# Sketched attention feeding a ReGLU layer on one core: key products of batch 0 on GpSimd alone, z sums that start with the rest, and loads that count as work in the plan

## The chip, the cores and the metric

One core of one Trainium2 chip. The metric is the device time of one execution in us; lower is better. Executions are marked fast or slow: slow is one that is over 1.5% above the fastest of the same kernel. The profile of a kernel is one execution; its span (first to last instruction) is 1.6 to 3.3 us below the execution's time in these runs.

## The reference, cut to what matters

```python
# q, k, v: (4 batches, 4 heads, 1088, 32); S1, S2: (8, 32); x: 4352 tokens of 128; d_ff 1536
def phi(x):                               # 64 features per token and head
    a = np.einsum('rd,bhsd->bhsr', S1, x)
    b = np.einsum('rd,bhsd->bhsr', S2, x)
    return np.einsum('bhsi,bhsj->bhsij', a, b).reshape(*x.shape[:-1], r * r)
q_p, k_p = phi(q), phi(k)
kv = np.einsum('bhsf,bhsd->bhfd', k_p, v)
z = np.sum(k_p, axis=2)
x = einsum('bhsf,bhfd->bhsd', q_p, kv) / (einsum('bhsf,bhf->bhs', q_p, z)[..., None] + 1e-06)
out = (np.maximum(x @ w_gate, 0.0) * (x @ w_val)) @ w_out      # x with its heads side by side
```

## The kernel before

The core works on 102 feed-forward units. Each unit is a gate and a val matmul, a ReLU on ScalarE, a product on VectorE (`ht`) and four out matmuls. They need x, which the attention makes group by group: group 0 (half of the first half of batch 0, units 0 to 5), group 1 (units 6 to 11), group 2 (units 12 to 23), then two groups for each later batch, and one for the last 64 tokens of every batch. All attention work of batch 0 up to the first x is start-up; that of the other batches is woven between the units.

The order of instructions is fixed when the kernel is built: a list scheduler (`plan`) gives each operation a duration, dependences, a level (its priority) and a gate (the unit at which it may be placed at the earliest), and emits the operations in the order of its own clock. On the chip an engine runs its operations in that order, and semaphores make it wait.

```python
def outer(eng, dst, ab, a0, b0, n, a=None):     # line 202 is in here: both inputs lie in SBUF
    eng.tensor_tensor(out=..., in0=a_src[..., None].to_broadcast(...),
                      in1=ab[:, :, None, b0:b0 + R].to_broadcast(...), op=ALU.mult)
# ... in add_k: key products, four of 128x512 per batch; VectorE shares them for batch 0
for c in range(0, GC, 2):
    for hf in range(2):
        dve = first and hf == 0
        phis.append(op("DVE" if dve else "POOL", 640 if dve else 1080, kb.phi, hf, ...))
# ... z: four sums over the chunks, then the rest (the last 64 tokens), then a mask, w, and its fill
for c in range(GC):
    zs.append(op("PE", 330, kb.z, c, ...))
zs.append(op("PE", 500, kb.z_rest, x, deps=(zs[-1], rest_t2), level=lv, **kw))
zd = op("DVE", 200, kb.zdiag, deps=(zs[-1],), level=lv, **kw)
# ... in plan: while TensorE would idle, matmuls of zeros (line 155, "fillers") keep it busy
gap = t - clock["PE"] if o.eng == "PE" else 0
if gap > WGAP and clock["PE"] < WARM_UNTIL:
    warm(int((gap - 100) / (57 if t > 7000 else 110)))
# ... leads in units: keys and queries of a batch are spread over units s-KA..s-KB and s-QA..s-QB
K0, KA, KB, QA, QB = 2, 35, 25, 20, 8
# ... loads: placed by gates and fixed times, no duration in the plan
op("ACT", 200, load_k, b, at=13500.0, gate=[0, -1, 4, 20][b])
op("ACT", 200, load_rest_q, b, gate=[0, 0, 10, 24][b])
```

The query side (`add_q`) is, per group: transpose of q, matmul with the sketches, transpose to `abq`, `bw` (a product of two parts of `abq`), `den`, `an`, the query product `qp` (line 202 again), transposes on TensorE, `num`, and x on ScalarE. Group 0 has `bw`, `an` and `qp` on VectorE; groups 1 and 2 have `bw` and `an` on VectorE and `qp` on GpSimd; the later groups have all three on GpSimd.

## Time and profile before

| | before |
|---|---|
| time, median of 3 (range) | 125.57 us (124.8 to 126.27) |
| span of the profiled execution (a fast one of 126.52 us, not among the three), mean granted clock | 123.9 us, 0.962 |
| mask of the z sums starts (VectorE, line 318) | 13.01 us |
| query product of group 0 starts (VectorE) | 17.38 us |
| first gate matmul (line 454) | 22.11 us |
| span minus first gate, called **middle** below | 101.8 us |

The mask, the query product and the first gate say how long the start-up takes; the middle says how well the rest runs, whatever the start did.

### The profile page before, as it was taken

To read this page: it belongs to the slowest core of one execution; us is meant where nothing else is said; L and a number is where in the kernel's file an instruction comes from. 1 tells how busy PE (TensorE), PEld (TensorE's weight loads), DVE (VectorE), ACT (ScalarE), POOL (GpSimd) and SP (SyncE) were. 2 spreads that over 40 slices of the span, in tenths; PEclk is the share of its full clock that TensorE was granted. 3 is DMA by queue.
4 is the path that set the end of the run, shared out by engine and by line. 5 is a ranking of instruction groups with operands and counts; after the bars stand their busy time and mean duration, and the time that the engine had idled before them with its cause. 6 is when DMAs were issued, how large, how long until landed. Compare 5 with 4: busy or idle time off the path is not lost.

```text
span 123.9 us, 2888 instructions
## 1 busy us (share of the span) xinstructions
PE 114.9 (93%) x1117; PEld 80.6 (65%) x1117; DVE 97.3 (78%) x198; ACT 81.3 (66%) x165; POOL 46.8 (38%) x62
## 2 busy tenths in 40 slices
PE   6994899889999999999999999999999999999940
PEld 6864748767877669765665568755655766667920
DVE  3589376587889889397999796788979998979940
ACT  4100004795865649698996578659979988989930
POOL 6959102600593179941510199117005404000000
PEclk9999559999999999999999999999999999999995
DMA  2999990554053507562002100120020011011022
GB/s 49 300 141 192 181 224 6 176 107 158 9 188 55 105 0 177 77 156 100 14 0 41 49 3 0 11 79 0 3 52 33 8 28 57 5 19 65 0 44 83
DMA packets 9521, 9.28 MB, mean 75 GB/s; under 512 B 3364, under 2 KB 7844, under 8 KB 9508
## 3 DMA queue, kind: packets, MB, share of 16 engines
q1 hardware_dynamic: 5228, 6.82, 18.7%
q0 software_dynamic: 4096, 2.25, 14.2%
q8 instruction: 8, 0.13, 0.4%
q10 hardware_dynamic: 184, 0.04, 0.1%
q14 instruction: 5, 0.04, 0.1%
HBM read 9.12 MB, written 2.23 MB: 92 GB/s over the span
## 4 chain that ended last, share of the span: by engine, by line
PE 74%; DVE 11%; DMA 5%; ACT 4%; issue 2%; SPq 1%; ACTq 0%
PE bank L454 16%; PE bank L481 16%; PE bank L466 15%; PE bank L372 8%; DVE ht L471 8%; PE bank L254 5%; DMA q_sb<-in_q_dram 5%; PE bank L409 3%; ACT g_sb L460 2%; PE bank L427 2%; PE bank L302 2%; PE bank L280 2%; PE bank L334 2%; PE bank L155 2%; PE bank L312 1%
## 5 line engine op out<-in xcount | busy, mean ns | idle before, releaser
L471 DVE TENSOR_TENSOR ht<-g_sb,bank 128x512 f16<-128x512 f16 x102 | 65.7, 676 | 11.3 <-ACT g_sb L460 5.3
L460 ACT ACTIVATE g_sb<-bank 128x512 f16<-128x512 f32 x102 | 60.0, 602 | 15.7 <-PE bank L454 13.7
L481 PEld LDWEIGHTS <-ht 128*128 128x128 f16 x408 | 30.3, 98 | 18.4 <-issue 2.0
L481 PE MATMUL bank<-wo,ht 128*128 128x128 f16 x408 | 39.3, 219 | 0.6 <-DVE ht L471 0.6
L454 PE MATMUL bank<-xT,wg 128*128 128x512 f16 (+1 forms) x120 | 38.7, 347 | 0.6 <-ACT xT L433 0.5
L466 PE MATMUL bank<-xT,wv 128*128 128x512 f16 (+1 forms) x120 | 38.3, 347 | 0.4 <-DVE ht L471 0.4
L202 POOL TENSOR_TENSOR qp<-an,abq 128x1024 f16<-128x1024 f32 (+1 forms) x9 | 15.8, 1757 | 8.7 <-DVE an L397 8.1
L202 POOL TENSOR_TENSOR kp<-abk 128x512 f16<-128x512 f32 x14 | 14.5, 1064 | 8.5 <-DVE abk L265 8.5
L384 POOL TENSOR_TENSOR bw<-abq 128x128 f32<-128x128 f32 (+1 forms) x7 | 3.1, 436 | 31.7 <-DVE abq L380 31.7
L466 PEld LDWEIGHTS <-wv 128*128 128x128 f16 x120 | 11.7, 99 | 3.3 <-issue 1.6
L454 PEld LDWEIGHTS <-wg 128*128 128x128 f16 x120 | 11.5, 100 | 3.3 <-issue 2.0
L372 PE MATMUL bank<-qt,wst 128*128 128x512 f32 (+2 forms) x26 | 11.4, 553 | 0.0
L416 ACT COPY pt<-bank 128x512 f16<-128x512 f16 x17 | 10.0, 596 | 1.4 <-PE bank L409 1.4
L254 PE MATMUL bank<-kt,sk 128*128 128x256 f32 x32 | 9.6, 396 | 0.0
L380 DVE STREAM_TRANSPOSE abq<-bank 128x512 f32<-128x512 f32 (+1 forms) x10 | 6.3, 633 | 2.9 <-PE bank L372 2.9
L155 PE MATMUL bank<-zero 128*128 128x128 f16 x88 | 7.5, 256 | 1.1 <-DVE maskw L142 1.1
L155 PEld LDWEIGHTS <-zero 128*128 128x128 f16 x88 | 6.7, 117 | 1.4 <-DVE maskw L142 1.1
L246 DVE STREAM_TRANSPOSE kt<-k_sb 128x512 f32<-128x512 f32 x8 | 5.5, 698 | 1.9 <-DMA k_sb<-in_k_dram 1.9
L324 ACT ACTIVATE kv<-bank 64x64 f16<-64x64 f32 x16 | 3.5, 218 | 5.2 <-PE bank L292 5.0
L433 ACT CAST xT<-bank 128x512 f16<-128x512 f32 (+1 forms) x10 | 5.3, 529 | 2.3 <-PE bank L427 2.2
L280 PEld LDWEIGHTS <-kp 128*128 128x128 f16 x64 | 4.2, 112 | 3.5 <-DVE kp L202 1.9
L280 PE MATMUL bank<-v_sb,kp 128*128 128x64 f16 x64 | 4.8, 206 | 1.8 <-DVE kp L202 1.8
(73 smaller groups left out, 98.7 us busy)
## 6 DMA issues: line engine op xcount, KB each, us to landing
q_sb<-in_q_dram SPq DMA_DIRECT2D x4, 544.0 KB, 7.5
out_dram<-o_sb SPq DMA_DIRECT2D x7, 256.0 KB
k_sb<-in_k_dram SPq DMA_DIRECT2D x3, 512.0 KB, 4.6
v_sb<-in_v_dram POOLq DMA_DIRECT2D x4, 256.0 KB, 5.9
k_sb<-in_k_dram SPq DMA_DIRECT2D x2, 256.0 KB
wg<-in_moe_w_gate_dram POOLq DMA_DIRECT2D x1, 384.0 KB, 7.3
wv<-in_moe_w_val_dram POOLq DMA_DIRECT2D x1, 384.0 KB, 8.6
wo<-in_moe_w_out_dram POOLq DMA_DIRECT2D x1, 384.0 KB, 10.2
```

Source lines behind the costliest of these rows:

```text
L155: nc.tensor.matmul(w_ps[:, 0:128], zero, zero, start=True, stop=True)
L202: eng.tensor_tensor(out=dst.rearrange("s x (i j) -> s x i j", i=R), in0=a_src[:, :, :, None].to_broadcast([dst.shape[0], n, R, R]), in1=ab ...
L254: nc.tensor.matmul(self.ps[h0][:, lo * n * 32:(lo + w) * n * 32].rearrange("p (c x) -> p c x", c=w), sk[:, hf].rearrange("p a b f -> p (a ...
L280: nc.tensor.matmul(self.m[:, p * 64:p * 64 + 64], self.kp[:, hf, c * H + 2 * p:c * H + 2 * p + 2].rearrange("s h f -> s (h f)"), v_sb[self ...
L372: nc.tensor.matmul(self.ps[:, i * w:(i + 1) * w], wst[:, b].rearrange("p h f -> p (h f)"), self.qt.rearrange("p x t -> p (x t)")[:, i * w: ...
L380: nc.vector.transpose(self.absb.rearrange("p x f -> p (x f)"), self.ps[:, 0:n * 128])
L416: nc.scalar.copy(out=self.pt[:, lo:hi], in_=self.ps[:, lo:hi])
L454: nc.tensor.matmul(g_ps[:, y * W:(y + 1) * W], wg[:, j], xT[:, self.col:self.col + W], start=True, stop=True)
L460: nc.scalar.activation(out=self.g_sb, in_=self.g_ps, func=ACTF.Relu)
L466: nc.tensor.matmul(self.v_ps[:, y * W:(y + 1) * W], wv[:, j], xT[:, self.col:self.col + W], start=True, stop=True)
L471: nc.vector.tensor_tensor(out=self.ht, in0=self.g_sb, in1=self.v_ps, op=ALU.mult)
L481: nc.tensor.matmul(o[:, s], self.ht[:, y * W + x * 128:y * W + (x + 1) * 128], wo[:, j], start=(j == 0 and s == 0), stop=(j == NJ - 1), sk ...
```

## The change

Its intent: VectorE, on the start-up's chain, loses the two key products of batch 0 to GpSimd. The rest's z sum goes ahead of the chunks, so that the mask needn't wait for it at the end. A load becomes work of a "DMA" stream in the plan, one load after the other, and what uses it depends on it. Leads and some durations are new. So are three buffers each for the results of gate and val instead of two and four, a higher level for the kv matmuls, kv's rest right after its first chunk, and two of the four kv copies of batch 0 on VectorE. Core of the diff (cut: the start and stop flags that follow from the new order, the copy's body, durations):

```diff
-    K0, KA, KB, QA, QB = 2, 35, 25, 20, 8
+    K0, KA, KB, QA, QB = 4, 37, 26, 24, 20
+    def load(ns, eng, t, fn, *args, **kw):
+        o = op(eng, t, fn, *args, **kw)
+        return op("DMA", ns, lambda: None, deps=(o,))
 # add_k
-                                  bank=(None,) if new else banks, level=lv, **kw))
+                                  bank=..., level=(3 if h0 == 0 else 2) if first else 0, **kw))
-                dve = first and hf == 0
-                phis.append(op("DVE" if dve else "POOL", 640 if dve else 1080, kb.phi, hf,
-                               nc.vector if dve else nc.gpsimd, c, 2, deps=tuple(t2s), ...))
+                phis.append(op("POOL", 1120 if first else 1080, kb.phi, hf, nc.gpsimd, c, 2,
+                               deps=tuple(t2s), level=lo_lv, **kw))
         zs = []
+        if first:
+            zs.append(op("PE", 500, kb.z_rest, x, deps=(rest_t2,), level=lv, bank=banks, **kw))
         for c in range(GC):
...
-        zs.append(op("PE", 500, kb.z_rest, x, deps=(zs[-1], rest_t2), level=lv, **kw))
+        if not first:
+            zs.append(op("PE", 500, kb.z_rest, x, deps=(zs[-1], rest_t2), ...))
...
-                cps.append(op("ACT", 210, kb.kvcopy, g, r, deps=(kvs[-1], *cps[-1:]), ...))
+                dve = first and g == 1
+                cps.append(op("DVE" if dve else "ACT", 230, kb.kvcopy, g, r, ..., deps=(kvs[-1],), ...))
 # loads of the later batches
-            lv = (op("POOL", 900, load_main, nc.gpsimd, v_sb[b], v, b, gate=[0, -1, 10, 20][b],
-                     at=13000.0), cast)
-            op("ACT", 200, load_k, b, at=13500.0, gate=[0, -1, 4, 20][b])
-            op("ACT", 200, load_rest_q, b, gate=[0, 0, 10, 24][b])
+            k_in = (load(1650, "ACT", 200, load_k, b, at=13500.0, gate=[0, -1, 4, 20][b]),)
+            q_in = (load(1800, "ACT", 200, load_rest_q, b, gate=[0, 0, 10, 24][b]),)
+            v_in = (load(1650, "POOL", 900, load_main, nc.gpsimd, v_sb[b], v, b,
+                         gate=[0, 0, 10, 20][b], at=13000.0),)
```

More of the change, by code (lines that the diff above doesn't have):

```diff
@@ L284, in kv @@
                         v_sb[self.b][:, 2 * p:2 * p + 2, cc * D:(cc + 1) * D],
-                        start=c == 0 and hf == 0 and p == 0, stop=False,
+                        start=c == 0 and hf == 0 and p == 0, stop=c == GC - 1 and hf == 1,
                         skip_group_check=True)
@@ L295, in kv_rest @@
                         vt[rows, 2 * p:2 * p + 2, e * D:(e + 1) * D],
-                        start=False, stop=e == E - 1, skip_group_check=True)
+                        start=False, stop=False, skip_group_check=True)
         def z(self, x, c):
-            if c == 0:
+            if x is not None:
                 self.zps = bank(x)[:, 0:64]
@@ L305, in z, with z_rest @@
                 ab.rearrange("s h (a f) -> s a h f", a=2)[:, :, :, R:2 * R],
-                start=c == 0, stop=False, skip_group_check=True)
-        def z_rest(self, rest):
+                start=x is not None, stop=False, skip_group_check=True)
+        def z_rest(self, x, rest):
+            if x is not None:
+                self.zps = bank(x)[:, 0:64]
             rows = slice(32 * self.b, 32 * self.b + 32)
@@ L313, in z_rest @@
                     self.zps[:, 0:32], ab.rearrange("s h f -> s (h f)"), ab[:, :, R:2 * R],
-                    start=False, stop=e == E - 1, skip_group_check=True)
+                    start=x is not None and e == 0, stop=e == E - 1, skip_group_check=True)
         def zdiag(self):
@@ L320, in zdiag, with kvcopy @@
                 in1=maskz.rearrange("p a h j -> p (a h j)"), op=ALU.mult)
-        def kvcopy(self, g, r):
-            nc.scalar.mul(
-                out=kv16[64 * r:64 * r + 64, self.b, r].rearrange("f (p g) d -> f p g d", g=2)[
-                    :, :, g],
-                in_=self.m[64 * g:64 * g + 64, 0:128].rearrange("f (p g d) -> f p g d", p=2, g=2)[
-                    :, :, g],
-                mul=KVSCALE)
+        def kvcopy(self, g, r, eng):
+            o = kv16[64 * r:64 * r + 64, self.b, r].rearrange("f (p g) d -> f p g d", g=2)[:, :, g]
+            i = self.m[64 * g:64 * g + 64, 0:128].rearrange("f (p g d) -> f p g d", p=2, g=2)[
+                :, :, g]
+            if eng is nc.scalar:
+                eng.mul(out=o, in_=i, mul=KVSCALE)
+            else:
+                eng.tensor_scalar(out=o, in0=i, scalar1=KVSCALE, scalar2=None, op0=ALU.mult)
         def w(self, x):
@@ L508, in __init__ @@
             self.holds, self.end = [], None
-    SEM = {"PE": 220.0, "ACT": 220.0, "DVE": 250.0, "POOL": 200.0}
+    SEM = {"PE": 220.0, "ACT": 220.0, "DVE": 250.0, "POOL": 200.0, "DMA": 2000.0, "SP": 2000.0}
     SLACK = (0.0, 60.0, 60.0, 0.0)
-    BUFS = {**dict.fromkeys(range(8), 1), "g": 2, "v": 4, "o": 2, "kt": 3, "qt": 3, "abk": 2, "abq": 2, "kp": 2,
+    BUFS = {**dict.fromkeys(range(8), 1), "g": 3, "v": 3, "o": 2, "kt": 3, "qt": 3, "abk": 2, "abq": 2, "kp": 2,
             "qp": 2, "ktr": 3, "pt": 2, "g_sb": 4, "ht": 8, "bw0": 1, "bw1": 1, "an": 2, "rd": 2, "zd": 2}
@@ L589, with add_rest @@
         units += [F(*grp, i) for i in range(NJ * grp[2] // 4)]
-    T0 = {"PE": 4700.0, "DVE": 2900.0, "ACT": 5300.0, "POOL": 7900.0}
+    T0 = {"SP": 4700.0, "DMA": 16500.0, "PE": 4700.0, "DVE": 2900.0, "ACT": 5300.0, "POOL": 7900.0}
     WGAP, WARM_UNTIL = 250.0, 16000.0
-    K0, KA, KB, QA, QB = 2, 35, 25, 20, 8
-    def add_rest(n, src, at, level, gate):
+    K0, KA, KB, QA, QB = 4, 37, 26, 24, 20
+    def load(ns, eng, t, fn, *args, **kw):
+        o = op(eng, t, fn, *args, **kw)
+        return op("DMA", ns, lambda: None, deps=(o,))
+    def add_rest(n, src, at, level, gate, loaded=()):
         x = Rest(n, src)
         kw = dict(level=level, gate=gate)
-        t1 = op("DVE", 360, x.t1, at=at, **kw)
+        t1 = op("DVE", 360, x.t1, at=at, deps=loaded, **kw)
         ab = op("PE", 240, x.ab, deps=(t1, sk_fill), bank=range(7), **kw)
@@ L604, in add_rest, with add_k @@
         return x, t2, phi
-    def add_k(b, rest, landed, gate, banks, loaded, behind):
+    def add_k(b, rest, landed, gate, banks, k_in, v_in, behind):
         kb = K(b)
@@ L613, in add_k @@
         for pr in range(2):
-            t1s.append(op("DVE", 620, kb.t1, pr, at=landed[pr], deps=tuple(t1s[-1:]), level=lv, **kw))
+            t1s.append(op("DVE", 620, kb.t1, pr, at=landed[pr], deps=(*t1s[-1:], *k_in), level=lv, **kw))
         n = 2 if first else 4
@@ L622, in add_k @@
                                   deps=(*t1s[h0 // 2:(h0 + n) // 2], sk_fill, *abs_[-1:], *behind),
-                                  bank=(None,) if new else banks, level=lv, **kw))
+                                  bank=(None,) if new else banks, level=(3 if h0 == 0 else 2) if first else 0, **kw))
                     abs_.append(new[-1])
@@ L630, in add_k @@
             for hf in range(2):
-                dve = first and hf == 0
-                phis.append(op("DVE" if dve else "POOL", 640 if dve else 1080, kb.phi, hf,
-                               nc.vector if dve else nc.gpsimd, c, 2, deps=tuple(t2s), level=lo_lv, **kw))
+                phis.append(op("POOL", 1120 if first else 1080, kb.phi, hf, nc.gpsimd, c, 2,
+                               deps=tuple(t2s), level=lo_lv, **kw))
         zs = []
+        if first:
+            zs.append(op("PE", 500, kb.z_rest, x, deps=(rest_t2,), level=lv, bank=banks, **kw))
         for c in range(GC):
-            zs.append(op("PE", 330, kb.z, c, deps=(*t2s, *zs[-1:]), level=lv,
+            zs.append(op("PE", 275, kb.z, c, deps=(*t2s, *zs[-1:]), level=lv,
                          bank=(None,) if zs else banks, **kw))
-        zs.append(op("PE", 500, kb.z_rest, x, deps=(zs[-1], rest_t2), level=lv, **kw))
+        if not first:
+            zs.append(op("PE", 500, kb.z_rest, x, deps=(zs[-1], rest_t2), level=lv,
+                         bank=(None,), **kw))
         zd = op("DVE", 200, kb.zdiag, deps=(zs[-1],), level=lv, **kw)
@@ L645, in add_k @@
         for c in range(GC):
-            kvs.append(op("PE", 280, kb.kv, c, bank=(None,) if kvs else banks,
-                          deps=(*phis[c // 2 * 2:c // 2 * 2 + 2], *kvs[-1:], *loaded), level=lo_lv, **kw))
-        kvs.append(op("PE", 300, kb.kv_rest, x, vt, deps=(kvs[-1], rest_phi), level=lo_lv, **kw))
-        hold("abk", t2s[0], kvs[-2])
-        hold("kp", t2s[0], kvs[-2])
+            kvs.append(op("PE", 240, kb.kv, c, bank=(None,) if kvs else banks,
+                          deps=(*phis[c // 2 * 2:c // 2 * 2 + 2], *kvs[-1:], *v_in), level=lv, **kw))
+            if c == 0:
+                kvs.append(op("PE", 300, kb.kv_rest, x, vt, deps=(kvs[-1], rest_phi), level=lo_lv, **kw))
+        hold("abk", t2s[0], kvs[-1])
+        hold("kp", t2s[0], kvs[-1])
         cps = []
@@ L653, in add_k, with add_q @@
             for r in range(2):
-                cps.append(op("ACT", 210, kb.kvcopy, g, r, deps=(kvs[-1], *cps[-1:]), level=lo_lv, **kw))
+                dve = first and g == 1
+                cps.append(op("DVE" if dve else "ACT", 230, kb.kvcopy, g, r,
+                              nc.vector if dve else nc.scalar, deps=(kvs[-1],), level=lv, **kw))
         hold("bank", kvs[0], cps[-1])
+        for c in cps[:-1]:
+            cps[-1].deps += (c,)
         return cps[-1], wf
-    def add_q(grp, n, kv, wf, landed, gate, fast, banks):
+    def add_q(grp, n, kv, wf, landed, gate, fast, banks, q_in):
         qk = Q(*grp, n)
@@ L663, in add_q @@
         rest = grp[0] == B
-        t1 = op("DVE", 560 if rest else 40 + 145 * c, qk.t1, at=landed, **kw)
-        ab = op("PE", 1000 if rest else 60 + 110 * c, qk.ab, deps=(t1, *wf), bank=banks, **kw)
+        t1 = op("DVE", 560 if rest else 40 + 145 * c, qk.t1, at=landed, deps=q_in, **kw)
+        ab = op("PE", 1000 if rest else 60 + 215 * c, qk.ab, deps=(t1, *wf), bank=banks, **kw)
         hold("qt", t1, ab)
@@ L735, in load_rest_q, with load_rest_kv @@
         load_q(nc.sync, b)
-        if b == 1:
-            load_rest(nc.sync, kr, k, range(B))
-            load_rest(nc.sync, vr32, v, range(B))
+    def load_rest_kv():
+        load_rest(nc.sync, kr, k, range(B))
+        load_rest(nc.sync, vr32, v, range(B))
     sketch = Sketch()
@@ L748 @@
     f0 = op("DVE", 420, fill_static, deps=(s_copy,), level=1)
-    rest0 = (*add_rest(32, kr0, 6000.0, 2, -1), vr0)
-    rest = (*add_rest(128, kr, 26000.0, 0, 7), vr)
-    cast = op("ACT", 400, lambda: nc.scalar.copy(out=vr, in_=vr32), gate=9, at=29000.0)
-    kvs, wfs, xs = [], [], []
+    rest0 = (*add_rest(32, kr0, 5500.0, 2, -1), vr0)
+    cast = None
+    kvs, wfs, xs, qs = [], [], [], []
     for b in range(B):
         s = start[b, 0, 2 if b == 0 else GC]
-        lv = ()
+        k_in = v_in = q_in = ()
         if b > 0:
-            lv = (op("POOL", 900, load_main, nc.gpsimd, v_sb[b], v, b, gate=[0, -1, 10, 20][b],
-                     at=13000.0), cast)
-            op("ACT", 200, load_k, b, at=13500.0, gate=[0, -1, 4, 20][b])
-            op("ACT", 200, load_rest_q, b, gate=[0, 0, 10, 24][b])
+            k_in = (load(1650, "ACT", 200, load_k, b, at=13500.0, gate=[0, -1, 4, 20][b]),)
+            q_in = (load(1800, "ACT", 200, load_rest_q, b, gate=[0, 0, 10, 24][b]),)
+            v_in = (load(1650, "POOL", 900, load_main, nc.gpsimd, v_sb[b], v, b,
+                         gate=[0, 0, 10, 20][b], at=13000.0),)
+        if b == 1:
+            kvr = load(600, "SP", 3000, load_rest_kv, gate=0)
+            rest = add_rest(128, kr, 0.0, 0, 7, (kvr,))
+            cast = op("ACT", 400, lambda: nc.scalar.copy(out=vr, in_=vr32), gate=9, deps=(kvr,))
+            rest = (*rest, vr)
+        if b > 0:
+            v_in += (cast,)
+        qs.append(q_in)
         n0 = len(ops)
-        kv, wf = add_k(b, rest if b else rest0, [(4300.0, 5300.0), (19500.0,) * 2, (0.0,) * 2, (0.0,) * 2][b],
-                       s - 40 if b > 1 else -1, range(7), lv,
+        kv, wf = add_k(b, rest if b else rest0, (4400.0, 5600.0) if b == 0 else (0.0, 0.0),
+                       s - 40 if b > 1 else -1, range(7), k_in, v_in,
                        (first_ab,) if b == 1 else ())
@@ L774 @@
                               2 if start[grp] == 0 else 1 if g0 else 0,
-                              range(7))
+                              range(7), q_in)
                 xs.append(x)
@@ L782 @@
     x, _ = add_q(groups[-1], len(xs), tuple(kvs), tuple(wfs), 0.0, start[groups[-1]] - 20, 0,
-                 range(7))
+                 range(7), sum(qs, ()))
     xs.append(x)
```

## The prediction

> **What bounds the kernel now.** I read the page's summary by slices first, then the chain of work that ended last, then the table of windows, and last the key outer products (line 202), because the chain passes through them.
>
> The slices are 3.1 us wide:
>
> ```profile
> PE   6994899889999999999999999999999999999940
> PEclk9999559999999999999999999999999999999995
> DMA  2999990554053507562002100120020011011022
> ```
>
> Counted from 0, from slice 9 (27.9 us) on TensorE is at 90% or more. The gaps are in the slices before (slice 3, 9.3 to 12.4 us, is at 4), and in slices 4 and 5 (12.4 to 18.6 us) its clock is halved. The windows say the same in us (columns: busy time and instructions of PE, PEld, DVE, ACT, POOL, then granted clock, DMA share, GB/s):
>
> ```profile
> 10.00:12.00 2.00, 0.78 (x6) 0.60 (x5) 2.00 (x1) 0.00 (x0) 2.00 (x3) 1.00 1.04 194
> 12.00:18.00 6.00, 5.12 (x26) 3.60 (x26) 3.36 (x11) 0.19 (x1) 0.71 (x1) 0.51 1.37 213
> 18.00:22.00 4.00, 3.63 (x53) 2.68 (x53) 2.56 (x11) 1.78 (x7) 1.15 (x2) 0.89 0.05 18
> 24.00:104.00 80.00, 79.53 (x766) 53.91 (x764) 68.66 (x128) 62.49 (x127) 32.95 (x36) 1.00 0.25 62
> ```
>
> Between 24 and 104 us TensorE has 0.5 us of idle time in 80; VectorE and ScalarE have 11 and 17 us. That stretch is bound by TensorE's amount of work. Between 10 and 22 us it did little, partly at half clock: the start is where time can be won. The chain there (start, us, what):
>
> ```profile
> 9.98 0.86 DVE kp L202
> 10.84 1.56 issue
> 12.40 0.68 DVE kp L202
> 13.08 0.14 DVE zd L318
> 13.23 0.04 issue
> 13.27 1.06 PE bank L334 x4
> ...
> 14.76 1.08 PE bank L372 x2
> ...
> 16.06 2.72 PE bank L372 x4
> 18.78 0.29 PE bank L292 x4
> 19.07 1.22 PE bank L155 x20
> 20.29 0.22 PE bank L409 x4
> ...
> 21.69 0.38 ACT xT L433
> 22.07 0.04 issue
> 22.11 0.38 PE bank L454 x2
> ```
>
> L454 at 22.11 is the first gate matmul of the feed-forward part; all before it is start-up. The end of that chain is the load of q for batch 0, two key products on VectorE, the masking of the z sums (L318), w (L334), the query sketches (L372, half clock), the rest matmuls of kv (L292), filler matmuls (L155), then transposes, num and x. The key products are the surprise:
>
> ```profile
> L202 POOL TENSOR_TENSOR kp<-abk x2: 1055/1057/1059, 9.8 to 10.9; 128x512 f16<-128x512 f32 x2
> L202 DVE TENSOR_TENSOR kp<-abk x2: 680/1620/2561, 9.9 to 12.4; 128x512 f16<-128x512 f32 x2
> ```
>
> The same product takes VectorE 0.68 us in one instance and 2.56 us in the other (minimum, median, maximum). The long one began at 9.92, 0.07 us after GpSimd began its own two, and ended at 12.48, one 0.68 us after GpSimd had finished them (11.93, near enough). VectorE lost 1.9 us, and the z mask, ready to run since 10.78, stood behind it in VectorE's order until 13.01.
>
> **What the Trainium skill says.** "SBUF — State Buffer", section "Who interferes with whom": a VectorE instruction with two SBUF inputs contends with a GpSimd instruction that reads SBUF, and the later one is blocked, not slowed. The trace agrees: 2.56 us beside GpSimd, 0.68 us when GpSimd was only issuing a DMA. "TensorE: Matmul & The Clock Gate", "Part 1: The HAM clock gate", puts the clock at half after a window of some 3.4 us without enough activity. The trace agrees in kind: after only fillers and small matmuls from 8.4 to 10.8 us and an idle 1.76 us, the granted clock is 0.50 from 12 to 18.6 us. "DMA: Bandwidth & Descriptors", "Issuing engines are not separate DMA queues", says DMAs of all issuers interleave on the same 16 engines. The page's DMA row is at 9 from 3 to 19 us, while k, q, v and the weights share them, which is what the change's single DMA stream models.
>
> **The change part by part.** The kernel's order of instructions comes from a list scheduler, so every edit of a duration or gate reorders. I worked the new start by hand, with the rules of the scheduler and with durations from the trace.
>
> (1) *Up to the second head pair's transpose: about 0.* The order becomes rest ahead of the second head pair on VectorE and TensorE. But the plan still places the first query transpose at 7.0 us, ahead of the rest's second transpose, and q lands at 7.94 us. VectorE will again stand there, and the second key transpose will again end near 9.07. GpSimd's first rest product stays at 8.8 to 9.9.
>
> (2) *Key products to GpSimd: removes 3.17 us from VectorE, adds two of 1.06 us to GpSimd.* GpSimd: 9.85 + 4 x 1.04 = 14.0 us, instead of 11.93 there and 13.08 on VectorE. So the keys themselves come 0.9 us later.
>
> (3) *z path, much earlier.* z_rest goes first (8.8 to 9.4), the four chunks follow and end at about 10.6. With VectorE free, the mask runs 10.6 to 10.8 (before: 13.01 to 13.22). w at full clock took 0.53 us in later batches, though up to 0.6 us of fillers may stand ahead of it: 11.6 us. The fill of wst to 11.8, first query sketch 12.4, its transpose (0.45) to 12.9. Before, that transpose ended at 16.33: 3.4 us won.
>
> (4) *A new wait.* The next operation, bw (L384), has two SBUF inputs, and GpSimd is busy with keys until 14.0. By the wait seen above it stands until about 14.0. From the start of bw to the end of the query product, before took 18.07 - 16.36 = 1.71 us: 15.7 us now, 2.35 us earlier than 18.07.
>
> (5) *The way from the query product to the first gate.* Before: 18.07 to 22.11, 4.04 us, because L372, L292 and 20 fillers stood ahead of the transposes on TensorE. From the transposes' start at 20.13 to the gate it was 1.98 us. Now kv has its keys at 14.0, so its last matmuls end near 14.8, and the four copies, two on ScalarE beside two on VectorE (0.22 each), end near 16 to 17, just beside the copy of the transposes. TensorE should be free at 15.7. Gate: 15.7 + 0.1 + 2.0 = 17.8; I add 0.2 for fillers or a copy of kv that come a little late: 18.0 us. **Gain 22.1 - 18.0 = 4.1 us.** Of it 2.35 come from the earlier query product, the rest from TensorE's queue, including its half clock (the two L372 groups took 3.8 us, against some 1.7 at full clock: 0.86 us for 512 columns later in the chain, and the two groups have 1024).
>
> (6) *Weights and loads.* wg, wv and wo land 7.3, 8.6 and 10.2 us after 5.35, 5.89 and 6.42: 12.7, 14.5 and 16.6 us, all ahead of a gate at 18.0. The v load of batch 1 moves from 11.88 to after the first gate, which can only help the weights. q of batch 1, issued after the first gate, was moved in some 3 us (issued 22.17, rates of 244 and 339 GB/s until 25); the plan now allows 4.2 us after its first gate.
>
> (7) *Steady part: the same work.* No matmul of keys, queries or feed-forward is removed, so with TensorE 99% busy the gain of the start passes through. Query work is released 24 to 20 units ahead instead of 20 to 8, so x is earlier and attention work no longer meets the last units. In 103.8 to 108.1 the chain goes over ScalarE and VectorE for 4.2 us, where some 0.5 us are lost. Against that, denser attention may cost something. Net: -0.2 us.
>
> Sum: 125.57 - 4.1 - 0.2 = 121.3 us.
>
> **The rivals.** *A: the wait moves.* GpSimd's longer run could block VectorE until well after 14.0, or TensorE's sparse work from 10 to 14 us could again halve its clock. For it: TensorE idled just 1.76 us before the fall. Against: its queue from 11.8 on holds sketches, kv and fillers. At half clock the remaining sketches, kv, transposes and first units would cost 1.5 to 2 us: 123 us. *B: hidden by later needs.* The units after the first six need x of the second group, whose query product on GpSimd now starts at about 18.7 and again waits for operations that GpSimd's reads block. I get x for unit 12 some 6.4 us after the first gate, against 7.2 before (29.29 - 22.11) and 12 units of 0.65 us: no stall. Were it wrong by 1.5 us: about 122.5. Or q of batch 1 lands after its planned transpose and holds VectorE's queue: 1 to 2 us, 122.5 to 123. *C: the start barely counts, reordering costs.* If bunched queries starve the feed-forward of banks or of VectorE, the middle loses 2 to 4 us: 124 to 126. TensorE's 0.5 us of idle in 80 shows the old order had no such trouble, and VectorE's 11 us of room speak against it.
>
> **Range and chances.** A, B and C together push upwards; downwards there is a gate near 17.3 and up to 1 us in the tail. 8 in 10: 119.6 to 123.4. The 2% line is 125.57 x 0.98 = 123.06; only A with B, or C, reach past it: faster 0.83, same 0.15, slower 0.02.
>
> **What would show it.** Right: first L454 between 17.5 and 18.6, last key product on GpSimd at about 14.0, z mask near 10.8, bw of the first group beginning to be held from about 13 and done just after 14, clock at 1.0 from 12 to 18, TensorE still about 99% busy afterwards, and the end as much earlier as the first gate. Wrong: a low clock digit in slices 4 to 6, gaps of TensorE in 18 to 30 us, or a first gate earlier by 4 us with an end that is not.

## The result, and the profile after

| | before | after |
|---|---|---|
| time, median (range), runs | 125.92 us (124.8 to 127.82), 4 | 120.5 us (120.22 to 120.68), 4 |
| span of the profiled execution, clock | 123.9 us, 0.962 | 118.5 us, 0.993 |
| z mask starts | 13.01 us | 10.15 us |
| query product of group 0 starts | 17.38 us | 14.43 us |
| first gate matmul | 22.11 us | 17.42 us |
| middle | 101.8 us | 101.1 us |

Ratio 0.9596 (95%: 0.9522 to 0.967), faster. A ratio is the mean time of one kernel's fast runs over that of the other's of the same rounds, so not quite the ratio of the medians in the table.

The slices of after (3.0 us wide), in the same rows as in the prediction:

```profile
PE   6999879999999999999999999999999999999920
PEclk9999999999999999999999999999999999999997
DMA  1999999594202740431002100020011012011021
```

Slice 3 had a 4 for TensorE before and has a 9; the clock has no low digit. The table of windows of after says the same in us:

```profile
10.00:12.00 2.00, 2.00 (x29) 1.85 (x27) 0.42 (x2) 0.00 (x0) 2.00 (x3) 1.00 1.05 184
12.00:18.00 6.00, 4.62 (x63) 3.40 (x62) 5.40 (x17) 1.73 (x7) 2.60 (x4) 1.00 1.33 189
24.00:104.00 80.00, 80.00 (x789) 53.83 (x788) 68.60 (x128) 63.42 (x130) 32.59 (x35) 1.00 0.20 53
```

From 12 to 18 us TensorE is busy for less time than before (4.62 against 5.12 us) but runs 63 matmuls instead of 26 (20 of them fillers), at a clock of 1.00 instead of 0.51. From 24 to 104 us it has no idle time left. In 10 to 12 us VectorE is busy 0.42 instead of 2.00 us: that is the held key product gone. The chain of after up to the first gate (start, us, what):

```profile
8.45 0.56 PE bank L315 x4
9.01 1.03 PE bank L303 x8
...
10.60 0.47 PE bank L338 x4
...
11.62 0.50 PE bank L376 x2
...
12.15 0.46 DVE abq L384
12.63 1.01 DVE bw L388
...
14.43 0.70 DVE qp L202
...
15.58 1.12 PE bank L155 x20
16.70 0.28 PE bank L431 x8
...
17.42 0.38 PE bank L458 x2
```

The rest's z sum (L315) and the chunks' (L303) come first, then w (L338), the sketches of group 0 (L376), and then VectorE. L458 is the first gate. One line is longer than it should be: `bw` takes 1.01 us. In VectorE's timeline (start, us, engine, line, operation) the two `bw` of the same shape in after are

```profile
12.63 1.00 DVE L388 TENSOR_TENSOR bw<-abq 128x64 f32<-128x64 f32 x1
15.66 0.21 DVE L388 TENSOR_TENSOR bw<-abq 128x64 f32<-128x64 f32 x1
```

and GpSimd's timeline has the key products of batch 0 in one piece, from 9.42 to 13.55 us, followed by a load's issue:

```profile
9.42 4.13 POOL L202 TENSOR_TENSOR kp<-abk 128x512 f16<-128x512 f32 x4
13.50 0.83 POOL L87 DMA_DIRECT2D v_sb<-in_v_dram  x1
```

The first `bw` started inside that piece and ended 0.08 us after it; the second had no GpSimd product beside it.

One part of the earlier start is not the change's. VectorE waits for the load of q before the first query transpose. The timelines of before, of after, and of after's second profile (e12 below) at that place:

```profile
7.97 0.45 DVE L362 STREAM_TRANSPOSE qt<-q_sb 128x256 f32<-128x256 f32 x1 [0.58 <-DMA q_sb<-in_q_dram]
7.54 0.45 DVE L366 STREAM_TRANSPOSE qt<-q_sb 128x256 f32<-128x256 f32 x1 [0.43 <-DMA q_sb<-in_q_dram]
8.16 0.45 DVE L366 STREAM_TRANSPOSE qt<-q_sb 128x256 f32<-128x256 f32 x1 [0.66 <-DMA q_sb<-in_q_dram]
```

The same kernel met q at 7.54 us in one execution and at 8.16 in the other, and its first gate came at 17.42 and 18.03.

### The profile page after: what moved, and what is told of

It reads as the page before. It is cut to its first block, busy times and chain, and to the rows that moved or that the text cites. A ratio compares the mean times of both kernels' runs of the same rounds, so it can differ in the third digit from the quotient of the medians.

```text
span 118.5 us, 2939 instructions
## 1 busy us (share of the span) xinstructions
PE 110.7 (93%) x1114; PEld 78.1 (66%) x1114; DVE 95.7 (81%) x198; ACT 79.8 (67%) x163; POOL 48.8 (41%) x64
## 4 chain that ended last, share of the span: by engine, by line
PE 78%; DVE 14%; issue 2%; ACT 1%; DVEq 1%
PE bank L485 15%; PE bank L458 15%; PE bank L470 15%; DVE ht L475 11%; PE bank L254 6%; PE bank L376 6%; PE bank L155 6%; PE bank L413 3%; PE bank L303 3%; PE bank L431 3%; PE bank L315 2%; PE bank L338 2%; PE bank L280 1%; DVE bw L388 1%; PE bank L224 1%
## 5 line engine op out<-in xcount | busy, mean ns | idle before, releaser
L464 ACT ACTIVATE g_sb<-bank 128x512 f16<-128x512 f32 x102 | 59.2, 607 | 13.0 <-PE bank L458 8.5
L485 PE MATMUL bank<-wo,ht 128*128 128x128 f16 x408 | 38.8, 219 | 0.4 <-DVE ht L475 0.4
L458 PE MATMUL bank<-xT,wg 128*128 128x512 f16 (+1 forms) x120 | 38.4, 347 | 0.5 <-ACT xT L437 0.5
L202 POOL TENSOR_TENSOR kp<-abk 128x512 f16<-128x512 f32 x16 | 16.5, 1061 | 6.3 <-DVE abk L265 6.3
L458 PEld LDWEIGHTS <-wg 128*128 128x128 f16 x120 | 11.9, 100 | 3.8 <-issue 2.2
L470 PEld LDWEIGHTS <-wv 128*128 128x128 f16 x120 | 11.8, 102 | 2.8 <-issue 1.4
L376 PE MATMUL bank<-qt,wst 128*128 128x512 f32 (+2 forms) x26 | 9.4, 475 | 0.0
L493 ACT ACTIVATE o_sb<-bank 128x512 f32<-128x512 f32 (+1 forms) x10 | 5.3, 532 | 3.3 <-PE bank L485 3.3
L747 ACT CAST k_sb<-wv 1x1 f32<-1x1 f16 x3 | 0.5, 179 | 9.0 <-DMA wv<-in_moe_w_val_dram 9.0
L413 PE MATMUL bank<-ident,qp 128*128 128x128 f16 x68 | 5.4, 219 | 1.1 <-DVE qp L202 0.9
## 6 DMA issues: line engine op xcount, KB each, us to landing
wo<-in_moe_w_out_dram POOLq DMA_DIRECT2D x1, 384.0 KB, 10.6
```

What stands on the lines that cost most here:

```text
L202: eng.tensor_tensor(out=dst.rearrange("s x (i j) -> s x i j", i=R), in0=a_src[:, :, :, None].to_broadcast([dst.shape[0], n, R, R]), in1=ab ...
L376: nc.tensor.matmul(self.ps[:, i * w:(i + 1) * w], wst[:, b].rearrange("p h f -> p (h f)"), self.qt.rearrange("p x t -> p (x t)")[:, i * w: ...
L413: nc.tensor.transpose(self.ps[:, k], self.qp[:, 2 * k:2 * k + 2].rearrange("s r f -> s (r f)"), ident)
L458: nc.tensor.matmul(g_ps[:, y * W:(y + 1) * W], wg[:, j], xT[:, self.col:self.col + W], start=True, stop=True)
L464: nc.scalar.activation(out=self.g_sb, in_=self.g_ps, func=ACTF.Relu)
L470: nc.tensor.matmul(self.v_ps[:, y * W:(y + 1) * W], wv[:, j], xT[:, self.col:self.col + W], start=True, stop=True)
```

## The experiments

Twelve runs in three groups, each group on one chip with its own runs of before (medians of before: 126.56, 126.37 and 125.41 us; so a run is compared by its ratio, or by spans within a group). My theory was: the gain is the start-up's, made by the key products' move, and the other parts only keep the middle from growing. The rivals: the order of the rest or the plan's DMA stream makes the gain; or the split of the keys doesn't matter, only the hole (the idle stretch) in TensorE's work and the halved clock that the plan's wrong duration led to.

### One part at a time

**e1**: before, with the key products on GpSimd alone.

```diff
-                dve = first and hf == 0
-                phis.append(op("DVE" if dve else "POOL", 640 if dve else 1080, kb.phi, hf, ...
+                phis.append(op("POOL", 1120 if first else 1080, kb.phi, hf, nc.gpsimd, c, 2, ...
```

> The kernel before with one edit: all four key products of batch 0 on GpSimd. Theory S (the start-up decides, and the keys on GpSimd are most of it): VectorE's 2.56 us product is gone, the z mask runs near 10.9 us instead of 13.0, the clock stays at 1.0 from 12 to 18 us, the first gate comes near 18.0 us (before 22.11), time 121 to 122 us. Rival M (the new leads, buffer counts and DMA stream, that is the middle, give a good part): first gate as above or later, time 123 us or more.

Measured: 122.45, 121.65, 121.61 us fast (one slow, 123.86, and that is the profiled one: first gate 19.88, middle 102.2). Ratio 0.9643 (0.9563 to 0.9723). The fast spans are 119.8 to 120.6 us, those of before on this chip 123.3 to 125.2. This one edit makes most of the gain. The start of a fast run was not profiled; with a middle of 102.2 their spans would put the first gate at 17.6 to 18.4 us (an estimate). The edit also gives the plan the true duration of these products, so it takes away the wait and the wrong number together; e9 takes them apart.

**e2**: after, with the keys split between VectorE and GpSimd again (the edit of e1 backwards).

> The kernel after with the keys of batch 0 split again between VectorE and GpSimd, all else of the change kept. Theory S: VectorE's first key product is again held behind GpSimd's (about 2.5 us instead of 0.68), the z mask comes after 12 us, first gate 19.5 to 21 us (after: 17.42), time 122.5 to 124.5 us. Rival M: the middle keeps most of the gain, time under 122 us.

Measured: 126.78 and 127.8 us fast, two slow; ratio 1.0155 (1.0043 to 1.0268): the gain is gone, and more. The key products (minimum, median, maximum in ns) are those of before:

```profile
L202 DVE TENSOR_TENSOR kp<-abk x2: 675/1565/2455, 9.7 to 12.2; 128x512 f16<-128x512 f32 x2
```

But the first gate is at 18.74 us, only 1.3 later than in after; the middle is 106.4, 5.3 longer, with a hole at 48 to 52 us (TensorE busy 1.6 of 4 us) and a clock of 0.55 to 0.59 in the 4 us behind it; as in e4 below, the keys of batch 2 run on GpSimd (from 43.18) ahead of a query product (47.28). So e2 doesn't measure the split alone: it also met a bad order later on. e6 takes that out.

**e3**: after, with the rest's z sum last again and the old levels and times for it.

```diff
-        if first:
-            zs.append(op("PE", 500, kb.z_rest, x, deps=(rest_t2,), level=lv, bank=banks, **kw))
...
-        if not first:
-            zs.append(op("PE", 500, kb.z_rest, ...
+        zs.append(op("PE", 500, kb.z_rest, ...
-    rest0 = (*add_rest(32, kr0, 5500.0, 2, -1), vr0)
+    rest0 = (*add_rest(32, kr0, 6000.0, 2, -1), vr0)
```

> The kernel after with the rest of k and the z sums of the rest in their old place (behind the second head pair, and last in the z sums). Theory S: VectorE's wait for q at about 7.5 us and GpSimd's key products until 13.55 us set the pace in both orders, so first gate 17.4 to 17.8 and time within 0.4 us of after (120.2 to 120.9). Rival O (the order of the rest is worth something by itself): first gate 18 or later, time 121.2 or more.

Measured: ratio 0.9562 (0.9472 to 0.9653), first gate 17.49, middle 101.1: no difference from after that these runs show. The order of the rest, which the change names in its title, is worth nothing here: the mask comes 0.7 us later (10.85), but GpSimd's keys begin at 9.49 (after: 9.42) and hold `bw` to their end in either order, so the delay only shortens that wait (0.38 instead of 1.00 us). The waiting for q that was expected to set the pace doesn't stand in e3's trace. Where `bw` isn't held, as in e8, the order was not tried.

**e4**: after, with the old leads.

```diff
-    K0, KA, KB, QA, QB = 4, 37, 26, 24, 20
+    K0, KA, KB, QA, QB = 2, 35, 25, 20, 8
```

> The kernel after with the five lead constants of before (2, 35, 25, 20, 8). Theory S: first gate unchanged at 17.4 us, and what the leads bring is the 0.7 us that the end gained beyond the first gate (5.4 against 4.7 us): time 120.9 to 121.4. Rival M: 122 us or more.

Measured: ratio 0.9863 (0.9793 to 0.9934). First gate 17.19, middle 105.9: the start is as good as after's, and 4.8 us are lost later. The slices (3.1 us wide) show where:

```profile
PE   6899889999999993799999999999999999999940
PEclk9999999999999998559999999999999999999995
```

TensorE is at 3 in slice 15 (46 to 49 us), and its clock halves behind it. GpSimd's timeline in e4, then in after, at that place:

```profile
41.24 4.14 POOL L202 TENSOR_TENSOR kp<-abk 128x512 f16<-128x512 f32 x4
45.34 1.95 POOL L202 TENSOR_TENSOR qp<-an,abq 128x1024 f16<-128x1024 f32 x1
```

```profile
40.33 1.96 POOL L202 TENSOR_TENSOR qp<-an,abq 128x1024 f16<-128x1024 f32 x1
42.24 4.14 POOL L202 TENSOR_TENSOR kp<-abk 128x512 f16<-128x512 f32 x4
```

In e4 the four key products of batch 2 run ahead of the query product that the next units (batch 1) need; in after it is the other way. x for those units comes at 49.80 us in e4 and 45.78 us in after. Before had the query product first too (44.53, the keys at 47.67).

### Is it that order on GpSimd?

**e5**: e4 with one dependence more: the key products of batches 2 and 3 wait in the plan for the first query product of the batch ahead.

```diff
+    ahead = {}
-    K0, KA, KB, QA, QB = 4, 37, 26, 24, 20
+    K0, KA, KB, QA, QB = 2, 35, 25, 20, 8
-                               deps=tuple(t2s), level=lo_lv, **kw))
+                               deps=(*t2s, *((ahead[b - 1],) if b > 1 else ())), ...))
+        if grp[1] == 0 and grp[0] > 0:
+            ahead[grp[0]] = phis[-1]
```

> The kernel with the old leads (the fourth run, 124.84 us) with one more dependence: the key products of batches 2 and 3 on GpSimd wait in the plan for the first query product of the batch before. Theory G (the hole of that run at 46 to 52 us is only GpSimd's order, 4.1 us of keys of batch 2 ahead of the 1.95 us query product of batch 1): the hole is gone, x of batch 1 comes some 4 us earlier (46 instead of 50 us), clock 1.0 throughout, time 120.4 to 121.4. Rival L (the old leads as such cost, by attention work spread too late): time 122 us or more.

Measured: 120.04 us in the one fast run, span 118.1 (e4: 122.2 to 123.1); three slow runs of 126.03 to 126.57. The profile is of a slow run: first gate 23.49, but middle 100.8. The hole is gone with the old leads kept. So the leads' worth is that order. One fast run is little, but the middle of the slow one says the same.

**The slow runs.** The profile of e5 let me see what slow is here. The matmuls of line 254 (ns: minimum, median, maximum), first e5, then after:

```profile
L254 PE MATMUL bank<-kt,sk x8: 633/635/796, 6.2 to 10.6; 128*128 128x256 f32 x8
```

```profile
L254 PE MATMUL bank<-kt,sk x8: 379/379/483, 5.4 to 7.8; 128*128 128x256 f32 x8
```

From the first matmuls until about 20.5 us TensorE ran at some half of its rate (ten fillers in 1.27 us at 14.5 us, against 0.72 in after), and the first gate came 6 us later; yet the record of the granted clock says 1.00 all that time (mean of the run 0.990). It doesn't go by kernel: of four executions each, three of e5 were slow, two of e2, e6, e7, e9, e10 and e11, one of e1 and e3, none of e4, e8 and the first four of after, and one of the second four. The profile fell on a slow run in e1, e5 and e10, and all three have these long matmuls, until about 20.5 us in e5 and e10 and only to 10 us in e1, whose slow run has a span 1.5 to 2.3 us longer than its fast ones; for the other slow runs no trace shows the cause. I did not find what decides it.

**e6**: after with split keys (e2) and the dependence of e5.

> The kernel with split keys (the second run, 128.38 us) with the same added dependence. Theory G: its hole in the middle goes and what is left is its later first gate (18.74 against 17.42), time 121.5 to 122.3. Rival (split keys cost beyond the first gate): 123 us or more.

Measured: 124.93 and 126.13 us fast (spans 122.6 and 123.7; two slow); ratio 1.0177 (0.9782 to 1.0572). First gate 20.43, middle 102.2. Against e2 the middle is 4.2 us shorter and the start 1.7 later (the clock dips here in slices 4 and 5, as before; in e2 it did not). Against after the span is 4.1 us longer, 3.0 of it in the start; against e12, whose q landed at nearly the same time (8.16, here 8.05), 3.5 and 2.4. That is the price of the split as the plan of before has it, with the wrong 640 ns and, in this execution, the clock's dip, but with the later hole taken out.

### Held by GpSimd, or only badly ordered?

**e9**: before, with the one wrong number put right: the plan gives the two split key products on VectorE the mean that the profile shows.

```diff
-                phis.append(op("DVE" if dve else "POOL", 640 if dve else 1080, kb.phi, hf,
+                phis.append(op("DVE" if dve else "POOL", 1620 if dve else 1080, kb.phi, hf,
```

> The kernel before with one number changed: the plan counts VectorE's key products of batch 0 as 1620 ns (what they took on average) instead of 640; both engines keep their keys. The plan then puts the z mask between the two products and fillers into TensorE's hole. Theory C (much of the start's loss was the hole and the halved clock behind it, not the place of the keys): clock 1.0 from 12 to 18 us, first gate 18.7 to 19.7, middle (span minus first gate) as before, 101 to 102.5, time 122 to 123.3. Theory S (the place of the keys is most of it): the product stays held to 12.5 us and the first gate is 20.5 or later, time 124 or more.

Measured: ratio 0.9775 (0.9694 to 0.9855); first gate 18.79 (before: 22.11), middle 102.1. The key products were still split and one still held (676 and 2261 ns). But the plan now knew it: it put the z mask between the two (12.07 us) and fillers into the wait. The slices of e9 (3.0 us):

```profile
PE   6998978999999999999999999999999999999940
PEclk9999999999999999999999999999999999999995
```

No halved clock. So 3.3 of the 4.7 us of the first gate came without moving any work, only with a true duration (some 0.3 of them because GpSimd's keys began 0.33 us earlier in this execution, at 9.52). The fast spans, 120.9 and 121.1 us beside 123.2 to 124.8, agree with that. This and e1 are two ways to the same hole, and their gains don't add up.

**e7**: after, with the sketches of group 0 transposed into PSUM instead of SBUF, and a copy of one factor to SBUF on ScalarE, so that `bw`, `an` and `qp` of that group have one SBUF input each; with e5's dependence.

```diff
+                self.absb = bank(x)[:, 0:n * 128].rearrange("p (x f) -> p x f", f=32)
+        def wcopy(self):
+            self.wc = a_sm.tile([128, self.n * H, R], FP32, name="wc")
+            nc.scalar.copy(out=self.wc, in_=self.absb[:, :, 2 * R:3 * R])
-                              in1=self.absb[:, :, 2 * R:3 * R], op=ALU.mult)
+                              in1=self.wc if wc else self.absb[:, :, 2 * R:3 * R], op=ALU.mult)
```

> The kernel after with the first query group's sketches written to PSUM (one ScalarE copy of a third of them to SBUF), so that its three products have only one SBUF input, and with the added dependence. If GpSimd's reads hold the bw product (1.00 us against 0.21 in the next group), bw now takes 0.2 to 0.25 us beside GpSimd's keys, and the query product ends near 14.8 instead of 15.1; first gate 16.9 to 17.2, time 119.8 to 120.4. If bw was held by something else (the bank, its order), it still takes about 1 us and the time is 120.4 to 121.

Measured: 123.01 and 122.51 us fast, two slow; ratio 0.9833 (0.9595 to 1.0071). `bw` took 0.19 instead of 1.00 us, beside the running key products: the wait was GpSimd's reads. The plan put the transpose of group 1 ahead of it, and q landed late in this execution (8.14 us): the query product began at 14.71 and the first gate at 17.45, like after's 14.43 and 17.42, where q landed at 7.54, but ahead of e12's 15.04 and 18.03, where it landed at 8.16. So by these profiles the start gained some 0.6 us, and the middle grew by 2.4: GpSimd's keys of batch 2 came at 47.31 (after: 42.24), and TensorE waited 0.79 us for them; the rest I did not trace. The cause is shown; the time was not won.

**e8**: e7, with the first query transposes planned at 8.3 us (about when q lands) instead of 7.0, and `bw` of group 1 behind the query product of group 0.

```diff
-                x, ab = add_q(grp, len(xs), (kv,), (wf,), 7000.0, -1 if g0 else ...
+                x, ab = add_q(grp, len(xs), (kv,), (wf,), 8300.0, -1 if g0 else ...
+                 deps=(wc or t2,) + (tuple(first_phi) if fast == 1 else ()), **kw)
```

> As the seventh, and batch 0's query transposes planned at 8.3 us instead of 7.0, so that VectorE doesn't stand waiting for q ahead of the rest's and the second pair's transposes; the next group's bw follows the first query product. Key products start about 0.5 us earlier and end near 13.0; first gate 16.2 to 16.8, time 119.2 to 120.0: a version that may beat after. If the wait for q was worth nothing, as the seventh.

Measured: 119.26 to 119.86 us, four fast runs; ratio 0.9578 (0.9482 to 0.9673; the verdict was "unclear", with four of the seven runs of before in that group marked slow). `bw` in VectorE's timeline:

```profile
12.90 0.18 DVE L395 TENSOR_TENSOR bw<-bank,wc 128x64 f32<-128x64 f32 x1
```

Query product 13.88, first gate 16.62 (after: 17.42), middle 101.4. Its spans, 117.5 to 118.1 us, are all below those of the fast runs of after (118.4 to 119.3), so it is the fastest version by its spans, by about 1 us (e5's one fast run, 118.1, lies beside it). The ratios' intervals overlap, and the two ran on different chips, so the size is uncertain.

### Fillers and the DMA stream

**e10**: after, without fillers past 8 us.

```diff
-    WGAP, WARM_UNTIL = 250.0, 16000.0
+    WGAP, WARM_UNTIL = 250.0, 8000.0
```

> The kernel after without fillers on TensorE later than 8 us in the plan (45 fewer matmuls of zeros). If the fillers keep the clock up: it falls to about 0.5 between 12 and 18 us, the sketches and kv take twice as long, first gate 18 to 19.5, time 121.5 to 123. If they only fill, nothing waits for them: first gate 17.0 to 17.4, time 120.0 to 120.5.

Measured: ratio 0.9701 (0.9615 to 0.9788), fast spans 119.7 and 120.5 us beside 119.1 to 119.3 of e12 on the same chip: the fillers are worth some 1 us. Mean clocks of those runs are 0.972 and 0.958 (e12: 0.988 to 0.996), so it seems to be paid in clock. Where the clock fell isn't shown: two of four were slow, and the trace is of one of those.

**e11**: after, with loads that have no duration in the plan, and the old fixed times for their users.

```diff
-        return op("DMA", ns, lambda: None, deps=(o,))
+        return o
-            rest = add_rest(128, kr, 0.0, 0, 7, (kvr,))
+            rest = add_rest(128, kr, 26000.0, 0, 7, (kvr,))
```

> The kernel after without the DMA stream in its plan: loads of batch 1 on are taken as landed at the fixed times of before. First gate unchanged at 17.4. The stream moves only where the loads' readers stand in the order: if the chip had them landed in time anyhow, span minus first gate stays 101 to 101.6 and the time is 120.2 to 120.9; if VectorE then stands waiting for q or k of batch 1, 121.5 or more.

Measured: 123.89 and 122.95 us fast, two slow; ratio 0.9831 (0.9742 to 0.992). First gate about 17.6, middle about 104.6. Its chain holds a load that after's doesn't:

```profile
17.62 4.38 DMA q_sb<-in_q_dram
```

VectorE stands before the transpose of q of batch 1 from the first units on, and the units' products stand behind it. The new lead would explain it (read from the plan's rules, not tried alone): batch 1 starts at unit 24, so with QA = 24 its query work may be placed at unit 0, where its load is only just issued; with QA = 20 it was unit 4. The stream is what makes the longer lead safe, worth 2 to 3 us here (spans 121.2 and 122.2 beside 119.1 to 119.3).

**e12**: after once more, beside e9 to e11.

> The kernel after, unchanged, on the chip of the two runs above, to compare them with and to see how often it meets the late release of the clock that other variants met at their start: all of 120.2 to 120.8 if never, single executions of 124 or more if so.

Measured: 120.82 to 121.45 us fast, one slow (126.25); ratio 0.9653 (0.9587 to 0.9719), first gate 18.03, middle 101.1. This is no better than e1's ratio on another chip; by spans e1 is about 1 us longer (119.8 to 120.6 against 118.4 to 119.3). What the other parts add on top of the keys' move lies between nothing and some 1.5 us, and is not settled more closely.

## Why the prediction was right or wrong, by its steps

The time came out 0.8 us below the predicted 121.3: the first gate was 0.6 earlier than its 18.0, and the middle shrank by 0.7 instead of 0.2. Most of the 0.6 is luck: q landed 0.43 us earlier in after's profile than in the one that the prediction reckoned from, and in e12, where it landed at 8.16, the same kernel has its keys from 10.04 to 14.16, the mask at 10.75 and the first gate at 18.03, nearly the predicted figures. For the same reason some 0.4 of the 4.7 us between the two profiles is not the change's.

- **(1) The order of the rest, about 0.** Right in size, and tested by e3. The reason given, VectorE's stand before q, is so in after's trace but not in e3's; there the length of GpSimd's keys makes the order worthless.
- **(2) Keys on GpSimd until 14.0.** 13.55: it began 0.4 earlier than assumed, since q landed earlier and the rest's product ran from 8.39 and not from 8.8. e1 shows that this move makes most of the gain.
- **(3) z mask at 10.6, first transpose of group 0 done at 12.9.** 10.15 and 12.60, in order and size; again earlier because q landed earlier.
- **(4) The new wait of `bw`.** Right: held from 12.63 to the end of the keys. e7 shows the cause, e8 that it can be removed.
- **(5) From the query product to the first gate, 2.3 us.** 15.12 to 17.42 is 2.3. Of the 4.7 us, 2.95 come from the earlier query product (it ended at 18.07) and 1.74 from the way behind it. One detail was wrong: the kv copies did not run two beside two. ScalarE's second waited 0.99 us for VectorE's first, and they alternated from 14.58 to 16.25. It cost next to nothing on the chain: fillers stood until 16.70, and the copy of the transposes, behind those copies on ScalarE, ended at 16.60.
- **(6) Loads.** The weights were in time. But "the v load of batch 1 moves to after the first gate" was wrong: it was issued at 13.50, right behind the keys. A gate orders an operation in the plan; on the chip nothing waits for it, so GpSimd, with its work done, issued the load.
- **(7) "The gain of the start passes through."** Right in direction (-0.7 instead of -0.2 us), incomplete in reason. It was argued from equal work and a busy TensorE. The same work lost 4.8 us in e4 and some 3.5 in e11 with an equally early start. In after it passes through only with the leads and the stream, which keep the supply of x ahead. But an earlier start alone doesn't need them: e1 and e9, with the old leads and no stream, kept middles of 102.2 and 102.1. So what e4 and e11 show are dangers of the order that the change as a whole makes (which of its parts makes them is open), and the new leads and the stream avoid these. The tail went as foreseen: from 99.0 to 112.3 us the chain of after is VectorE's unit products alone, about 0.655 us apart, with no attention work left beside them.

**The rivals.** A: `bw` was held as long as the keys ran and no longer, and the clock held. The fillers differ less in number (85, before 88) than in place: 20 stand between 9.8 and 11.7 us, where before had none. e10 suggests that without them some clock is lost. B and C did not occur in after; e11 is B's waiting for q, e4 is C's starving, by way of GpSimd's order rather than of banks. Split keys with a true plan (e9) are a rival that I had not put forward: most of the start's loss was the plan's ignorance of the wait and only partly the wait.

## What to carry to other kernels

In a statically ordered kernel, an operation that the trace shows far over its planned time costs twice: the wait itself, and the order that was planned around the wrong number; put the measured duration into the plan first (e9: 2.3% from one number). Where two engines block each other's reads, as VectorE and GpSimd do here, try to give a chain's work to one of them (e1: 3.6%), and check what the longer run of it then holds. And after any gain in a start-up, subtract the first useful instruction from the span: if that difference grows, the supply behind it is out of order, and taking a part out of the finished change (e4, e11) says what it guards, which is not what it adds alone (e1).

## What the Trainium skill lacked or had wrong

- "SBUF — State Buffer", "Who interferes with whom": that the later instruction is blocked agrees (2.56 us before, 1.00 us for `bw` in after, 0.18 us with one input in PSUM in e8). It doesn't say that the blocked one doesn't get in between two GpSimd instructions that follow each other: before, VectorE's product stood from 9.92 to about 11.8 us over both of GpSimd's (9.85 to 11.93).
- "TensorE: Matmul & The Clock Gate", "Part 1: The HAM clock gate": it gives an idle window of some 3.4 us for the fall to half clock. Before fell to 0.51 in 12 to 18 us with 1.76 us of full idleness and thin work ahead of it, and e4's fell in the second of two idle times of 0.94 and 1.16 us (48 to 49 us: 0.68 on the mean, then 0.50); a lower limit on how little is enough is missing.
- The same section warns that recorded clock events can be unreliable. The runs show one form of it: line 254 at a median of 635 instead of 379 ns, with a recorded clock of 1.00, until some 20.5 us (e5). Reading the duration of one known matmul is the surer test.
